# A transformer block in float32: the first stage's loads, warm-up and first tile rearranged

## The chip, the cores and the metric

The kernel runs on one core of a Trainium2 chip. A core has five engines that run side by side: TensorE (PE, matrix products into the accumulators in PSUM; its weight loads are shown apart as PEld), VectorE (DVE), ScalarE (ACT), GpSimd (POOL) and SyncE (SP, which here issues transfers). Sixteen DMA engines move data between the device's memory and the on-chip memory (SBUF). Each engine works through its own list of instructions in order, and waits on semaphores for the others. The metric is the device's time for one execution, in microseconds (us); smaller is better.

## The reference

The computation is linear attention without softmax, followed by an MLP mixer over tokens and then over channels. There are 8 batches, 8 heads, 576 tokens and 64 numbers a head; all is float32.

```python
kv = np.einsum('bhsd,bhse->bhde', k, v)
out = np.einsum('bhsd,bhde->bhse', q, kv)
rms = np.sqrt(np.mean(out * out, axis=-1, keepdims=True) + 1e-06)
attn = (out / rms * g_norm).astype(np.float32)

x = attn.transpose(0, 2, 1, 3).reshape(B, S, H * D)      # (8, 576, 512)
h = np.maximum(x.transpose(0, 2, 1) @ w_tok1, 0.0) @ w_tok2
u = x + h.transpose(0, 2, 1)
h2 = np.maximum(u @ w_ch1, 0.0) @ w_ch2
return (u + h2).astype(np.float32)
```

`w_tok1` is 576 x 256, `w_tok2` 256 x 576, `w_ch1` 512 x 1536, `w_ch2` 1536 x 512. The weights reach the kernel as pairs of 32-bit words for each number, and the kernel makes float32 of them ("decoding").

## The kernel before

The work has two parts. The first does attention and token mixing for pairs of batches, four pairs in all; the second does channel mixing, with products that are split further. The change touches only the first pair ("the first stage") and the loads ahead of it.

**The order is written out by hand.** Every instruction is recorded with `keep` (`tc.keep_in_program_order`), so each engine runs its instructions in the order in which the program issues them. That order comes from lists of short names: `start` for the first pair, `middle` and `steady` for the others. `play` (L1257) walks through the names and calls the function of each. The names that matter here, with S a batch of the pair (side), C a chunk of 256 tokens (0 and 1 of side 0, 2 and 3 of side 1, 4 the 64 last tokens of both), T one of its two tiles of 128 tokens, H a half:

- `kvSH` and `eSH` (L373, L387): k-by-v for four heads of one batch (20 products of 128x64, over five groups of rows), and its copy out of PSUM into `kvp`
- `aCT` (L395): one tile of q by kv, 4 products of 128x128; `a40` is the tile of the last tokens (`ps_r`)
- `gCT`, `qCT`, `tCH` (L444, L455, L469): times g into x (DVE), the square (ACT), the sum of squares of each head (DVE)
- `mC`, `rC`, `iC` (L477 to L493): mean, root and inverse for a whole chunk: on DVE, on ACT, and four small instructions on DVE
- `dCT`, `sCT` (L509, L502): x times the inverse, on DVE in one instruction or on ACT in eight
- `hSTj` (L541): x of group j times `w_tok1` (two weight passes of a 128x512 product each), for the first token product; `hr` adds the last tokens, `uN` is the second token product
- `wNK` (L162 to L192): decoding of block N in four steps: 1 on ACT (two instructions), 2, 3 and 4 on DVE. Blocks 0 and 1 hold groups 0, 1 and 2, 3 of `w_tok1`; block 2 its last rows; blocks 3 and 4 are `w_tok2`
- `lS`, `lqS`, `lrS`: the loads of the next pair; `jN` (L1341) N products on an identity matrix whose result nobody uses; `gs` (L1298) spreads g over the partitions with a product

A float32 product shows as two instructions of PE in the profile.

**Loads.** All go through `dma` (L123), nearly all on SyncE's queue. A load may be issued only when the load eight places earlier has landed. Before `start`, the program issues (L1276 to L1284): k of batch 0 on SyncE and v of batch 0 on ACT (each its rows, 1024 KB, and two remainders of 64 KB), q of batch 0 (`qT`, 1024 KB), blocks 0 and 1 of `w_tok1` (512 KB each), k and v of batch 1, q of batch 1, the last tokens of both q (`qR`), and the last rows of `w_tok1`. GpSimd sets the unused rows of k and v to zero (L1286) and then makes the identity; the row of g is loaded on ACT's queue (L1296).

**PSUM.** Three pools of 2 KB banks: `o` (2), `kv` (2) and `h` (4). In the first pair the two `kv` banks are set to zero and filled side by side (`zeroed`), the tiles of q by kv take `o`, and the accumulators of token mixing, the warm-up products and `ps_g` take `h`.

## Time and profile before

| | us |
|---|---|
| median of 3 runs (771.4 to 772.31) | 771.54 |
| the profiled execution | 771.12 |
| its span, first to last instruction | 769.3 |
| TensorE busy / idle in the span | 759.4 / 9.9 |
| DVE busy | 642.5 |
| ACT busy | 277.4 |
| first `ps_j` product / first `ps_kv` product | 3.34 / 8.81 |
| first `ps_g` / first `ps_o` / first `ps_h` product | 11.83 / 12.19 / 19.35 |
| first `ps_kv` product of batch 1 | 21.67 |
| first `ps_u` product | 47.20 |

The granted clock of TensorE is 0.999 over the span. The DMA engines are busy in over nine tenths of most slices of the first 80 us. The times of the rows in the lower half are from the profile's timeline, and count from the first instruction of the span.

### The profile page before, as it was taken

The numbers are of one execution on the slowest core, as the hardware profiler recorded it, in microseconds if no ns is written. First come the engines' busy times: TensorE is split into PE (matmuls) and PEld (weight loads), VectorE is DVE, ScalarE is ACT, GpSimd is POOL, SyncE is SP. The second block draws the span as 40 slices with busy tenths as digits, with TensorE's granted clock in tenths as the row PEclk, the third lists the DMA queues.
The fourth block names the chain that finished last, engine by engine and source line by source line (L and its number), as shares of the span: only waits on it lengthen the run. The fifth ranks groups of instructions, "written<-read, shape, count | busy, mean of one in ns | idle before, by whom it ended". The sixth has DMA issues, their size and how long they took to land.

```text
span 769.3 us, 12678 instructions
## 1 busy us (share of the span) xinstructions
PE 759.4 (99%) x4676; PEld 612.3 (80%) x4676; DVE 642.5 (84%) x945; ACT 277.4 (36%) x556; POOL 112.3 (15%) x125
## 2 busy tenths in 40 slices
PE   7999999999999999999999999999999999999998
PEld 6665555445888888888888888888888888888887
DVE  3868897997767779899969889987998996798996
ACT  3555575764210233511244242123352223325221
POOL 1003020213410000002240001042000218000204
PEclk9999999999999999999999999999999999999999
DMA  9999998499699786589998577999659879955679
GB/s 339 366 366 370 373 372 301 151 318 342 251 286 339 271 282 191 164 270 207 216 236 251 158 224 216 255 188 267 202 148 290 172 220 208 207 145 157 151 200 119
DMA packets 137677, 188.26 MB, mean 245 GB/s; under 512 B 48658, under 2 KB 95250, under 8 KB 135570
## 3 DMA queue, kind: packets, MB, share of 16 engines
q1 hardware_dynamic: 101744, 167.54, 68.9%
q0 software_dynamic: 34816, 18.36, 16.1%
q10 hardware_dynamic: 1058, 1.57, 0.6%
q8 instruction: 37, 0.61, 0.3%
q14 instruction: 22, 0.18, 0.1%
HBM read 138.28 MB, written 49.15 MB: 244 GB/s over the span
## 4 chain that ended last, share of the span: by engine, by line
PE 97%; DMA 2%; SPq 0%; issue 0%; DVE 0%
PE ps_d L136 28%; PE ps_b L136 19%; PE ps_a L136 19%; PE ps_u L136 8%; PE ps_h L136 8%; PE ps_v L136 5%; PE ps_c L136 3%; DMA v_in<-in_v_dram 2%; PE ps_kv L136 2%; PE ps_o L136 2%; PE ps_w L136 2%; SPq L124 0%; PE ps_r L136 0%; DVE xs L127 0%
## 5 line engine op out<-in xcount | busy, mean ns | idle before, releaser
L136 PE MATMUL ps_d<-ui,w 128*128 128x256 f32 x504 | 118.6, 379 | 0.0
L136 PEld LDWEIGHTS ps_d<-ui,w 128*128 128x128 f32 x504 | 95.9, 190 | 12.9
L133 ACT COPY ps_d<-ps_a 128x768 f32<-128x768 f32 (+1 forms) x56 | 32.0, 572 | 200.2 <-PE ps_a L136 197.2
L127 DVE TENSOR_TENSOR v<-v,v 128x1536 f32<-128x1536 f32 (+2 forms) x70 | 103.2, 1482 | 0.3
L136 PE MATMUL ps_b<-sv,w 128*128 128x256 f32 x324 | 78.9, 380 | 0.0
L136 PE MATMUL ps_a<-v,w 128*128 128x256 f32 x324 | 78.8, 379 | 0.0
L1206 POOL DMA_DIRECT2D out_dram<-us x24 | 26.7, 1833 | 291.8 <-ACT p L133 286.2
L136 PEld LDWEIGHTS ps_b<-sv,w 128*128 128x128 f32 x324 | 61.3, 190 | 8.8 <-issue 0.6
L136 PEld LDWEIGHTS ps_a<-v,w 128*128 128x128 f32 x324 | 61.7, 190 | 8.2
L136 PE MATMUL ps_u<-h,w_tok 128*128 128x512 f32 (+1 forms) x160 | 64.7, 599 | 0.0
L136 PE MATMUL ps_d<-v,w 128*128 128x256 f32 x258 | 62.7, 379 | 0.0
L130 ACT ACTIVATE v<-v 128x768 f32<-128x768 f32 (+1 forms) x54 | 42.6, 822 | 55.1 <-DVE v L127 52.3
L136 PE MATMUL ps_h<-x,w_tok 128*128 128x512 f32 x128 | 57.8, 600 | 0.7 <-DVE w_tok L190 0.7
L1206 POOL DMA_DIRECT2D out_dram<-r x40 | 41.3, 1927 | 102.0 <-ACT p L133 80.3
L136 PE MATMUL ps_d<-sv,w 128*128 128x256 f32 x228 | 55.4, 379 | 0.0
L136 PEld LDWEIGHTS ps_d<-v,w 128*128 128x128 f32 x258 | 49.0, 190 | 6.5
L136 PEld LDWEIGHTS ps_u<-h,w_tok 128*128 128x128 f32 (+1 forms) x160 | 25.6, 179 | 31.1 <-issue 26.7
L136 PEld LDWEIGHTS ps_d<-sv,w 128*128 128x128 f32 x228 | 43.4, 190 | 5.8
L136 PE MATMUL ps_a<-uT,w 128*128 128x256 f32 x192 | 46.7, 379 | 0.0
L136 PEld LDWEIGHTS ps_h<-x,w_tok 128*128 128x128 f32 x128 | 23.4, 190 | 27.1 <-issue 24.1
L136 PE MATMUL ps_b<-ui,w 128*128 128x256 f32 x168 | 40.8, 379 | 0.0
L136 PEld LDWEIGHTS ps_a<-uT,w 128*128 128x128 f32 x192 | 36.5, 190 | 4.9
(169 smaller groups left out, 1288.0 us busy)
## 6 DMA issues: line engine op xcount, KB each, us to landing
w<-parts SPq DMA_DIRECT2D x168, 384.0 KB
w<-parts SPq DMA_DIRECT2D x56, 192.0 KB
uT<-blocks SPq DMA_DIRECT2D x36, 256.0 KB
k_in<-in_k_dram SPq DMA_DIRECT2D x8, 1024.0 KB
qT<-in_q_dram SPq DMA_DIRECT2D x8, 1024.0 KB
out_dram<-x POOLq DMA_DIRECT2D x16, 512.0 KB, 7.0
v_in<-in_v_dram SPq DMA_DIRECT2D x7, 1024.0 KB
raw<-in_moe_w_ch_dram SPq DMA_DIRECT2D x8, 768.0 KB
```

The costliest lines, as they stand in the source:

```text
L127: keep(engine.tensor_tensor(out=o, in0=a, in1=b, op=op))
L130: keep(nc.scalar.activation(o, a, AF.Relu))
L133: keep(nc.scalar.copy(o, a))
L136: keep(nc.tensor.matmul(*a, **kw))
L1206: keep(nc.gpsimd.dma_start(to, t()[ds(b * Q, Q), at].rearrange("p n l j -> p n (l j)"), accum_op=ALU.add))
```

## The change

In the changed program:

- v of batch 0 is loaded on SyncE's queue too; for batch 0 the rows of k and v come first and the four remainders after them. g's row is loaded on GpSimd's queue, ahead of the memsets there. Block 0 of `w_tok1` is loaded and decoded in two halves (`first_rows`), the first right after batch 0 of k and v, the second after batch 1; block 1 follows the second half. q of batch 0 is loaded in two halves of 256 tokens.
- `kv00` and `kv01` are each split into the four groups of rows (`ka`) and the remainder (`kb`); `gs` stands between.
- The warm-up takes 21 products in place of 12, on a matrix of ones that DVE sets, and four more ahead of `a00`; the eight products ahead of `h000` are gone.
- The first tile's x no longer comes from `g00` and `d00`. kv times g is made on DVE for both halves (`eg0`, `eg1`), a product of q with it (`ag`) follows `a01`, and `dg` multiplies that by the inverse. The two tiles of chunk 0 have statistics of their own (`m00`, `r00`, `i00`; `m01`, `r01`, `i01`).
- `e01` moves from DVE to ACT; tile 1's scaling from ACT (`s01`) to DVE (`d01`), tile 11's from DVE (`d11`) to ACT (`s11`). Tiles `a30` and `a31` take the banks of `kv`, `a11` one of `h`. In the second half of `start` the products `h002`, `h012` come after `a31`.

```diff
-        queues = (nc.sync, nc.sync if b else nc.scalar)
-        for dst, t, e in zip((k_in[b % 2], v_in[b % 2]), (k, v), queues):
-            dma(dst[:, :J], t[b, :LO].rearrange("(p j) e -> p j e", j=J), e)
-            for n in range(0, HF, Q):
-                dma(dst[n:n + Q, J], t[b, LO + n:LO + n + Q].rearrange("(r e) d -> e r d", e=8), e)
+        pairs = ((k_in[b % 2], k), (v_in[b % 2], v))
+        if b:
+            for dst, t in pairs:
+                load_rows(dst, t, b)
+                load_rem(dst, t, b)
+        else:
+            for f in (load_rows, load_rem):
+                for dst, t in pairs:
+                    f(dst, t, b)
...
-            dma(qT[b], q[b].rearrange("(c p) s -> p c s", p=P)[..., :LO])
+            for n in range(0, LO, LO if b else LO // 2):
+                at = ds(n, LO if b else LO // 2)
+                dma(qT[b][..., at], q[b].rearrange("(c p) s -> p c s", p=P)[..., at])
...
+    def get_tok1_half(j):
+        return block(DTOK, lambda raw: [(raw, words(moe_w_tok1)[ts(j, P)])], w_tok1[0][:, j])
...
+        def evict_gain(half):
+            if not half:
+                sq["kvg"] = work.tile([P, H, D], F32, name="kvg", tag="sq", bufs=3)
+            keep(nc.vector.tensor_mul(sq["kvg"][:, 4 * half:4 * half + 4],
+                                      kv_ps[0, half].rearrange("p i (h d) -> p (i h) d", d=D),
+                                      g_sb.to_broadcast([P, 4, D])))
+
+        def attend_gain():
+            o = ps["h"].tile([P, DM], F32, name="ps_og", tag="h")
+            bank["g"] = o
+            for hp in range(HP):
+                matmul(o[:, ts(hp, P)], lhsT=qT[0][:, hp, ts(0, P)], rhs=sq["kvg"][:, 2 * hp:2 * hp + 2], start=True, stop=True)
 
         def attend_tile(c, t):
             side = c // 2
-            o = ps["o"].tile([P, DM], F32, name="ps_o", tag="o")
+            n = "kv" if c == 3 else "h" if (c, t) == (1, 1) else "o"
+            o = ps[n].tile([P, DM], F32, name="ps_o", tag=n)
...
+            if alone(c):
+                g = h
+                stat[g] = [stats.tile([P, H, 1], F32, name=name + str(h)) for name in ("ms", "root", "inv")]
+                keep(nc.vector.tensor_reduce(stat[g][0], sq[c, h], axis=AX.X, op=ALU.add))
+                return
...
+        def scale_first():
+            X[pair, 0] = xps[pair % 2].tile([P, 2, DM], F32, name="x", tag="x2", bufs=4)
+            of = lambda t: t.rearrange("p (k h d) -> p k h d", h=2, d=D)
+            keep(nc.vector.tensor_mul(of(X[pair, 0][:, 0]), of(bank["g"]), inv_of(0, 0).to_broadcast([P, HP, 2, D])))
...
+    first_rows = [get_tok1_half(j) for j in range(2)]
...
+    dma(g_row, bass.AP(tensor=g_norm.tensor, offset=g_norm.offset, ap=[[0, 1], list(g_norm.ap[0])]), nc.gpsimd)
     load(0)
+    first_rows[0][0]()
     load_q(0)
-    for block in tok1[:2]:
-        block[0]()
     load(1)
+    first_rows[1][0]()
+    tok1[1][0]()
     load_q(1)
...
+    keep(nc.vector.memset(ones, 1.0))
...
-        "j12 kv00 e00", "kv01 gs e01 l0", "a00 g00 q00", "a01 g01 q01 t00 t01 m0 w01",
-        "a10 w02 r0 i0 w03 d00 w04 q10 w30 w40 lq0", "a11 q11 s01 g10 g11 w11 j8",
-        "h000 h010 w12 w13 w14 t10 t11 m1 r1", "kv10 e10", "kv11 e11 i1 d10 d11 l1", "h001", "a20 q20", "h011",
-        "a21 q21 g20 g21 t20 t21 m2", "h002 h012 r2", "a30 g30 i2 d20 q30", "a31 q31 s21 g31 t30",
+        "j21 ka00 ka01 gs kb00 e00 kb01 e01 eg0 eg1 l0 w01 w02 w03 w04 j4",
+        "a00 q00 t00 m00 r00 i00", "a01 q01", "ag dg g01 t01 m01", "a10 q10", "a11 q11 r01 i01 w51 d01 w52 w53 w54",
+        "w30 w40 lq0 h000 h010", "kv10 e10 g10", "kv11 e11 g11 w11 t10 t11 m1 r1 w12 w13 i1 w14 d10 l1", "h001", "a20 q20", "h011",
+        "a21 q21 s11", "a30 q30", "a31", "h002 h012 g20 g21 t20 t21 m2 r2 i2 d20 g30 q31 s21 g31 t30",
         "h003 h013 t31 m3",
         "a40 q40 r3 i3 d30 s31 g40 t40 m4 r4 w21 i4 d40 lr0 lr1"]
...
     def keep_warm(n):
 
-        o = ps["h"].tile([P, DM], F32, name="ps_j", tag="h")
+        if n > 4:
+            late["junk"] = ps["h"].tile([P, DM], F32, name="ps_j", tag="h")
         for _ in range(n):
-            matmul(o[:, :P], lhsT=ident, rhs=ident, start=True, stop=True)
+            matmul(late["junk"][:, :P], lhsT=ones, rhs=ones, start=True, stop=True)
```

More of the change, by code (lines that the diff above doesn't have):

```diff
@@ L9 @@
 from concourse.dve_ops import ADD32_U16LIMBS
-from concourse.masks import make_identity
 F32 = mybir.dt.float32
@@ L97 @@
           for n, b in (("o", 2), ("kv", 2), ("h", 4))}
-    ident = inp.tile([P, P], F32, name="ident")
+    ones = inp.tile([P, P], F32, name="ones")
     g_sb = inp.tile([P, 1, D], F32, name="g_sb")
-    g_row, ones = (inp.tile([1, n], F32, name=name) for n, name in ((D, "g_row"), (P, "ones")))
+    g_row = inp.tile([1, D], F32, name="g_row")
     w_tok1 = [tokw.tile([P, 2, DTOK], F32, name=f"w_tok1{i}") for i in range(J // 2)]
@@ L139, with load_rows, load_rem @@
     qT, q_rest = {}, {}
+    def load_rows(dst, t, b):
+        dma(dst[:, :J], t[b, :LO].rearrange("(p j) e -> p j e", j=J))
+    def load_rem(dst, t, b):
+        for n in range(0, HF, Q):
+            dma(dst[n:n + Q, J], t[b, LO + n:LO + n + Q].rearrange("(r e) d -> e r d", e=8))
     def load(b):
@@ L164, in decode, with high, low, scale @@
         bits = dst.bitcast(U32)
-        def scale():
+        def high():
             keep(nc.scalar.activation(dst, raw()[..., 1].bitcast(F32), AF.Prelu,
                                       scale=2.0 ** -112, alpha=2.0 ** 32))
-            low = raw()[..., 0]
-            keep(nc.scalar.activation(low, low, AF.Copy, scale=2.0 ** -29))
+        def low():
+            t = raw()[..., 0]
+            keep(nc.scalar.activation(t, t, AF.Copy, scale=2.0 ** -29))
+        def scale():
+            high()
+            low()
         def scale_leaves():
@@ L190, in add @@
             keep(nc.vector._custom_dve(ADD32_U16LIMBS, out=o, in0=o, in1=flat().bitcast(U16)[..., 2 * leaves:][..., :2]))
-        return scale_leaves if leaves else scale, clamp, shift, add
+        return scale_leaves if leaves else scale, clamp, shift, add, high, low
     def words(w):
@@ L371, in attention, with kv @@
         whole = pair == 0
-        def kv(side, half):
+        def kv(side, half, js=range(JJ)):
             kk, vv = k_in[side], v_in[side]
-            if whole:
+            if js[0]:
+                o = kv_ps[side, half]
+            elif whole:
                 o = kv_ps[side, half] = zeroed[half]
@@ L378, in kv @@
                 o = kv_ps[side, half] = ps["kv"].tile([P, 2, P], F32, name="ps_kv", tag="kv")
+            split = len(js) < JJ
             for i in range(2):
-                for j in range(JJ):
+                for j in js:
                     for h in range(2):
@@ L384, in kv @@
                                rhs=vv[:, j, at],
-                               start=(j == 0), stop=(j == JJ - 1), skip_group_check=True)
+                               start=(j == 0 and not (split and i)), stop=(j == JJ - 1), skip_group_check=True)
         def evict(side, half):
@@ L389, in evict @@
             o, i = kvp[side][:, 2 * half:2 * half + 2, :n], kv_ps[side, half][:, :, :n]
-            if whole and side == 0:
+            if whole and side == 0 and half == 0:
                 keep(nc.vector.tensor_copy(o, i))
@@ L460, in group @@
             return next(g for g in groups if c in g)
+        alone = lambda c: whole and c == 0
         def stats_of(c):
@@ L495, in inv_of @@
         def inv_of(c, t):
+            if alone(c):
+                return stat[t][2].rearrange("p (k h) o -> p k h o", h=2)
             inv = stats_of(c)[2]
@@ L519, in attention @@
             for h in range(2):
-                steps |= {f"kv{s}{h}": do(kv, s, h), f"e{s}{h}": do(evict, s, h),
+                steps |= {f"ka{s}{h}": do(kv, s, h, range(J)), f"kb{s}{h}": do(kv, s, h, range(J, JJ)),
+                          f"kv{s}{h}": do(kv, s, h), f"e{s}{h}": do(evict, s, h),
                           f"l{s}": do(load, 2 * pair + 2 + s)}
@@ L532, in attention @@
                 steps |= {f"{n}{c}{t}": do(f, c, t) for n, f in zip("spd", (scale, scale_pool, scale_vector))}
+        if whole:
+            for h in range(2):
+                steps |= {f"m0{h}": do(mean, h), f"r0{h}": do(sqrt, h), f"i0{h}": do(invert, h)}
+                steps |= {f"eg{h}": do(evict_gain, h), "ag": attend_gain, "dg": scale_first}
         for g in groups:
@@ L1250, in stream @@
         for n in range(len(blocks)):
-            clamp, shift, add = blocks[n][2:]
+            clamp, shift, add = blocks[n][2:5]
             if n + 1 < len(blocks):
@@ L1293 @@
     keep(nc.scalar.activation(root, root, AF.Sqrt))
-    make_identity(nc, ident)
-    keep(nc.gpsimd.memset(ones, 1.0))
-    dma(g_row, bass.AP(tensor=g_norm.tensor, offset=g_norm.offset, ap=[[0, 1], list(g_norm.ap[0])]), nc.scalar)
     def spread_g():
         o = ps["h"].tile([P, DM], F32, name="ps_g", tag="h")
-        matmul(o[:, :D], lhsT=ones, rhs=g_row, start=True, stop=True)
+        matmul(o[:, :D], lhsT=ones[:1], rhs=g_row, start=True, stop=True)
         copy(g_sb[:, 0], o[:, :D])
     start = [
[4 rows of a table removed]
[4 rows of a table added]
         "h003 h013 t31 m3",
@@ L1333 @@
     mixings.append(token_mixing(B // 2 - 1, range(2, 9), (0, 1)))
-    more = {f"w{n}{k}": f for n, b in enumerate(tok1 + tok2) for k, f in enumerate(b)}
+    more = {f"w{n}{k}": f for n, b in enumerate(first_rows[:1] + tok1[1:] + tok2 + first_rows[1:]) for k, f in enumerate(b)}
     more |= {f"f{n}": b[0] for n, b in enumerate(channel)}
@@ L1341, in keep_warm @@
     def keep_warm(n):
-        o = ps["h"].tile([P, DM], F32, name="ps_j", tag="h")
+        if n > 4:
+            late["junk"] = ps["h"].tile([P, DM], F32, name="ps_j", tag="h")
         for _ in range(n):
-            matmul(o[:, :P], lhsT=ident, rhs=ident, start=True, stop=True)
-    more |= {f"j{n}": do(keep_warm, n) for n in (8, 12)}
+            matmul(late["junk"][:, :P], lhsT=ones, rhs=ones, start=True, stop=True)
+    more |= {f"j{n}": do(keep_warm, n) for n in (4, 5, 21)}
     more["gs"] = spread_g
```

## The prediction

> **What bounds the kernel now.** I read the page's first part and its chain of work first, then the same chain cut to the first 60 us, then what TensorE waited for over the whole span.

> ```profile
> PE   759.4 (99%) x4676; PEld 612.3 (80%) x4676; DVE 642.5 (84%) x945; ACT 277.4 (36%) x556; POOL 112.3 (15%) x125
> ...
> PE 97%; DMA 2%; SPq 0%; issue 0%; DVE 0%
> ...
> 0.75 7.97 DMA v_in<-in_v_dram
> ...
> 11.65 9.89 DMA v_in<-in_v_dram
> 21.54 0.14 issue
> 21.67 2.55 PE ps_kv L136 x80
> 24.23 1.06 PE ps_h L136 x2
> 25.28 1.09 PE ps_o L136 x8
> ...
> PE ps_j L136 <- POOL ident masks.py:199: 3.3, 1, 3.3
> PE ps_kv L136 <- DMA v_in<-in_v_dram: 1.5, 3, 0.8
> PE ps_h L136 <- DVE w_tok L190: 0.7, 1, 0.7
> PE ps_o L136 <- ACT sq L457: 0.6, 1, 0.6
> ```

> TensorE is the bound, and all its waits (6.1 us) lie before 21.67 us. From there to the end it never waits, so the time is settled by when this dense part begins. The chain says what lets it begin: not TensorE's early work but the landing of the second v (v1) at 11.65 + 9.89 = 21.54. All that TensorE does earlier (warm-up, kv of k0 and v0, tiles a00 to a11, two ps_h products) hangs beside that chain.

> Next I looked at what could bind soon after v1: the second q (qT1), which a20 needs. Its landing shows on SyncE, which may issue a load only when the load eight places earlier is down; v2's rows wait for qT1:

> ```profile
> 21.64 2.09 SPq L124 DMA_DIRECT2D k_in<-in_k_dram  x3
> 25.12 2.39 SPq L124 DMA_DIRECT2D v_in<-in_v_dram  x3
> ...
> SPq L124 <- DMA qT<-in_q_dram: 1.4, 1, 1.4
> ...
> 25.21 0.97 PEld L136 LDWEIGHTS ps_o<-kvp,qT 128*128 128x128 f32 x8 [0.76 <-ACT kvp L133]
> ```

> The first two lines are SyncE's timeline, the third its waits from 23.4 to 25.5 us, the last the timeline at a20. SyncE waited 1.4 us for qT and went on at 25.12; a20's weights began to load at 25.21. (The line puts the wait on ACT's copy of kvp, done by 24.63; the later release is qT1.) So a20 stands at two limits at once: v1 plus the products before it, and qT1's landing at about 25.1. This decides the case.

> The transfers themselves, in stretches (the last two numbers: busy share of the DMA engines, GB/s):

> ```profile
> 1.50:3.00 1.50, 0.00 (x0) 0.00 (x0) 0.00 (x0) 0.00 (x0) 1.37 (x5) 1.00 0.72 153
> 3.00:7.50 4.50, 4.16 (x22) 4.16 (x23) 0.00 (x0) 1.49 (x2) 0.43 (x2) 1.00 1.01 404
> 10.00:14.00 4.00, 4.00 (x82) 3.87 (x79) 1.39 (x3) 0.21 (x1) 0.00 (x0) 1.00 1.02 325
> 14.00:20.00 6.00, 4.73 (x37) 4.11 (x36) 5.66 (x15) 5.53 (x16) 0.00 (x0) 1.00 1.01 410
> 22.00:25.00 3.00, 3.00 (x79) 2.38 (x74) 2.55 (x9) 0.85 (x3) 0.00 (x0) 1.00 1.18 273
> ```

> From 3 us to 25 us the engines are full: nothing arrives earlier except by changing places with something else.

> **The change, part by part.** *Loads.* Sizes from the page: 1024 KB of rows and 2 x 64 KB of remainder for each k or v, 1024 KB a qT, 512 KB a block of w_tok1. Before, v1 ends after 2304 (k0, v0) + 1024 (qT0) + 1024 (two blocks) + 2304 (k1, v1) = 6656 KB, and qT1 after 7680. In the changed program's order on SyncE v1 ends after 2304 + 256 (half a block) + 1024 + 2304 = 5888 KB; then come half a block, a whole block and qT1, which again ends after 7680. So v1 comes 768 KB (786 kB) earlier: 1.95 us at 404 GB/s, 2.4 at 325. I take 1.95, since the window just ahead of it runs at 410: v1 at 19.6, bounds 19.1 to 19.6. qT1 stays at 25.1, because the same bytes lie ahead of it. qT0 now goes in two halves, whose contiguous pieces are half as long. No row times such pieces. Lower bound 0 (same bytes); upper, the fall from 404 (long pieces) to 325 GB/s (pieces of qT and w_tok1) once more, to 261: 1049 kB take 4.0 instead of 3.2 us, +0.8. I take 0.1, as both rows show full engines. A gain is possible too: see the first rival.

> v0 moves from ACT's queue behind k0 on SyncE's. Its rows issue about 0.45 us later (three k issues took 2.07 us), but k0 then has the engines to itself and the remainders no longer come between. The 2097 kB of rows: 230 kB by 3.0 us, the rest at 404 GB/s, so 7.6, and 7.9 with 0.3 for landing, against 0.75 + 7.97 = 8.72. g_row moves to GpSimd's queue, ahead of the four memsets there; those end about 2 us later, near 5, and are needed at 10. The page's GpSimd transfers land 5.7 to 7.1 us after issue, so g_row lands near 8 and is first used at 9.9.

> [...]

> *TensorE's early work.* Warm-up: 42 passes in place of 24, started by a memset on DVE near 1.1 instead of GpSimd's identity at 3.34. Before, 24 passes took 4.62 us; passes ran at 213 ns until 6.7 us and at 111 later. If the switch again takes 3.4 us, 42 passes end at 1.1 + 3.4 + 26 x 0.111 = 7.4; if it waits until 6.7, at 8.4. Then kv of the rows (64 passes, 2.0 us as at 9.82 to 11.83) 7.9 to 9.9; ps_g 0.36; remainders 16 passes, 0.5, to 10.75; four warm-up products 0.9 to 11.65; a00 and a01 1.78 (the row at 14.83) to 13.4; the new product with kv times g, 8 passes, 0.9, to 14.3; a10 and a11 to 16.1.

> Tile 0's own statistics: a00 is complete at 12.75; square 0.60, reduce 0.68, then mean, root and inverse 1.42 (23.39 to 24.81 before) to 15.55; one scaling straight from the new product, 0.69, to 16.3. The two kv-times-g multiplies (half of a 0.69 tile each) are done by 11.9, and the half decode (0.29 + 0.29 + 0.43) by 13.0, both beside TensorE's work. So h000 starts at 16.35 instead of 19.35: 3.0 us earlier, done at 18.1.

> *Where these 3 us go.* kv10 waits for v1 until 19.7 (idle 1.6), ends at 22.2, h001 (0.86) at 23.1. Then a20 waits for qT1 until 25.2 (idle 2.1). From a20 on both programs have the same products up to h100 (16 of ps_o, 8 of ps_r, 5 of ps_h), only in another order. The part that never waits thus starts at 25.2 to 25.3, where it started before.

> *DVE and ACT behind it.* Costing these at nothing needs cover. DVE's d10 comes after w11 on ACT, itself behind the copy of kv11 (done 22.7): w11's first half 23.4, w12 and w13 to 24.7, inverse 25.7, w14 26.4, d10 27.1. From there to the last decode of w_tok2 DVE has 8 multiplies (5.5), 5 reduces (3.2), 3 statistics (4.3) and decodes (1.2 + 1.85 + 1.85), together 17.9, plus about 1.2 us in which tile 2's root waits on ACT behind s11, now ACT's, and q30: 46.2. TensorE's u0 needs it at 47.2. Before, that decode ended at 44.89: the cover shrinks from 2.3 to 1.0 us. If it went, each missing us would be added to the time. PSUM: a30 and a31 take kv's banks, free since the copies at 22.7; the next kv needs them at 37.9, and DVE reads a31 by 34.9.

> *Sum.* Waits before 21.67: -3.0 us of early work, given back as 1.6 + 2.1 of new waits; later qT1 +0.1. Span 769.3 + 0.1 = 769.4. The profiled execution took 771.12, 1.8 more than its span: 771.2. The median of the runs shown, 771.54, is 0.4 above it, so as a median 771.6; as a gain on qT1 is likelier than a larger loss, I say 771.5.

> **The rivals.** *The transfers run better.* qT1's landing includes the two stretches at 325 and 273 GB/s. If the first does not recur, 1.30 MB at 404 take 0.8 us less; if the second does not, 0.82 MB take 1.0 less. Then qT1 lands at 23.3 and a20 follows h001 directly. For it: the order changes just there. Against: the blocks of w_tok1 and the short rows of qR, which stand in those stretches, move along with qT1. The gain is 0.9 to 1.9 us, more than the cover of 1.0 left by DVE only if v1, and so DVE, comes earlier too: 769.7 (-1.8).

> *The clock falls (slower).* Place: the two new waits of 1.6 and 2.1 us before kv10 and a20. If TensorE returns to 213 ns a pass for the 3.4 us that it took to leave it, 1.7 us of work are lost: 773.2. It decides from the idle time at which the clock is taken back. Known rows: idle 0.85 us at 7.96 left passes at their fast rate. For it: the waits are over twice as long; against: 3.4 us of work lie between them.

> [...]

> *It does not do what it says.* g_row lands late on GpSimd's queue and holds the remainders of kv. That counts only past 13.5 us (1.6 + 2.1 us of cover): twice its expected time. With other late loads behind the halves of qT0: 773 or more.

> **How the numbers follow.** qT1 binds, no change: 0.63, at 771.5 (own range 770.4 to 772.6: +-0.8 for qT1, +-0.3 for the runs). Transfers run better: 0.21, 769.7. Clock: 0.11, 773.2. Late loads: 0.05. A measurement of this kernel tells about 0.2% (1.5 us) from no change, so faster is below 770.0: three quarters of the better-transfers case and a little of the first, 0.18. Slower is above 773.1: 0.11 + 0.05 + 0.02 = 0.18. Same: 0.64. The range takes in part of both sides: 769.8 to 773.2.

> **What would show it.** Right: ps_h first at about 16.4; ps_kv of the second pair released by v_in near 19.6; TensorE idle some 2 us before a20; SyncE's wait for qT ending near 25.1; then no wait up to the end. Wrong: a20 well before 24 (then transfers ran better, and I look for a wait at u0 on DVE); passes of 213 ns after 18 us (clock); ps_kv or ps_g held past 10 us by g_row.

## The result and the profile after

The changed kernel takes 773.78 us (median of 13 executions, 771.93 to 776.54) against 771.40 (13 executions, 770.91 to 772.86) for the kernel before: ratio 1.0024, 95% interval 1.0014 to 1.0035. It is slower, by some 1.9 us by this ratio of all executions and by 2.4 us between the medians (the executions fall into groups, see below). The median is above the predicted range (769.8 to 773.2).

The profiled execution took 774.07 us with a span of 772.0, against 771.12 and 769.3. First the page's busy time and chain:

```profile
PE 763.5 (99%) x4694; PEld 615.0 (80%) x4694; DVE 643.8 (83%) x954; ACT 278.3 (36%) x560; POOL 112.2 (15%) x123
...
PE 96%; DMA 3%; DVE 0%; SPq 0%; issue 0%
```

TensorE has only 18 passes more but is busy 4.1 us longer. Its waits over the whole span (us in total, times, longest):

```profile
PE ps_o L135 <- DMA qT<-in_q_dram: 2.1, 1, 2.1
PE ps_j L135 <- DVE ones L1348: 1.1, 1, 1.1
PE ps_kv L135 <- DMA v_in<-in_v_dram: 0.4, 1, 0.4
PE ps_h L135 <- DVE w_tok L208: 0.2, 1, 0.2
```

The waits fell from 6.1 to 3.8 us, and the largest is the predicted one for qT1, to the tenth. TensorE's timeline (start, length, instructions, and in brackets the idle time before them and what ended it) shows the same:

```profile
16.82 1.98 PE L135 MATMUL ps_h<-x,w_tok 128*128 128x512 f32 x4
19.22 2.77 PE L135 MATMUL ps_kv<-v_in,k_in 128*64 128x64 f32 x80 [0.41 <-DMA v_in<-in_v_dram]
22.16 1.12 PE L135 MATMUL ps_h<-x,w_tok 128*128 128x512 f32 x2 [0.18 <-DVE w_tok L208]
25.39 1.50 PE L135 MATMUL ps_o<-kvp,qT 128*128 128x128 f32 x8 [2.10 <-DMA qT<-in_q_dram]
26.69 1.91 PE L135 MATMUL ps_h<-x,w_tok 128*128 128x512 f32 x2
28.39 3.33 PE L135 MATMUL ps_o<-kvp,qT 128*128 128x128 f32 x24
```

a20 starts at 25.39, 0.15 us later than in the kernel before (25.24). So far nothing is lost. But two passes of ps_h take 1.91 us here against 1.12 at 22.16: from a20 on TensorE works at about half speed. The stretches of the timeline (after the times and the busy time of TensorE and its weight loads come DVE, ACT, GpSimd, then the granted clock, DMA share and GB/s) name the reason:

```profile
19.16:22.58 3.42, 3.18 (x81) 2.85 (x82) 2.30 (x6) 1.60 (x5) 0.00 (x0) 1.00 1.06 372
22.58:25.99 3.41, 1.31 (x7) 0.63 (x6) 3.27 (x10) 1.16 (x3) 0.00 (x0) 1.00 1.17 271
25.99:29.40 3.41, 3.41 (x12) 2.38 (x12) 2.17 (x5) 0.60 (x1) 0.00 (x0) 0.50 0.99 318
29.40:32.82 3.42, 3.42 (x24) 2.73 (x23) 2.05 (x4) 2.79 (x10) 0.00 (x0) 1.00 1.01 404
```

The clock stands at 0.50 from 25.99 to 29.40, 3.41 us, and at 1.00 before and after. The stretches are cut where this profile's clock records change: it rose at 5.51 us, fell at 25.99, six steps of 3.413 us later, and rose again at 29.40, one step on. In the stretch that ends where the clock falls TensorE was busy for 1.31 of 3.41 us, 38%.

Lining up the products of both profiles gives the account of the 2.67 us by which the span grew: 0.15 at a20; 1.67 more by ps_r (35.09 against 33.27), about half of 3.41; nothing from there to the last product (767.11 against 765.27); and 0.83 behind the last product, where the span goes on for 4.58 us in place of 3.75. Another 0.28 lies outside the span (2.10 in place of 1.82 between span and execution).

In that end SyncE's stores wait longer for each other. Of SyncE's waits in the last nine us, the one for an earlier store of xg lasts at most 2.0 us, where the kernel before had 1.1 in its last nine (the first line is the changed kernel's, the second that of the kernel before):

```profile
SPq L123 <- DMA out_dram<-xg: 2.9, 2, 2.0
SPq L124 <- DMA out_dram<-xg: 1.6, 2, 1.1
```

### The profile page after: what moved, and what is told of

The parts are those of the page before. It is cut to its first block, busy times and chain, and to the rows that moved or that the text cites. A ratio compares the mean times of both kernels' runs of the same rounds, so it can differ in the third digit from the quotient of the medians.

```text
span 772.0 us, 12727 instructions
## 1 busy us (share of the span) xinstructions
PE 763.5 (99%) x4694; PEld 615.0 (80%) x4694; DVE 643.8 (83%) x954; ACT 278.3 (36%) x560; POOL 112.2 (15%) x123
## 4 chain that ended last, share of the span: by engine, by line
PE 96%; DMA 3%; DVE 0%; SPq 0%; issue 0%
PE ps_d L135 28%; PE ps_b L135 19%; PE ps_a L135 19%; PE ps_u L135 8%; PE ps_h L135 8%; PE ps_v L135 5%; PE ps_c L135 3%; PE ps_o L135 2%; PE ps_w L135 2%; PE ps_kv L135 2%; DMA qT<-in_q_dram 1%; DMA k_in<-in_k_dram 1%; DMA v_in<-in_v_dram 1%; PE ps_r L135 0%; DVE xs L126 0%; SPq L123 0%
## 5 line engine op out<-in xcount | busy, mean ns | idle before, releaser
L135 PEld LDWEIGHTS ps_h<-x,w_tok 128*128 128x128 f32 x128 | 23.7, 192 | 27.1 <-issue 24.6
```

What stands on the lines that cost most here:

```text
L135: keep(nc.tensor.matmul(*a, **kw))
```

## The experiments

Theory: the 2.1 us of waiting in front of a20 leave one window of 3.41 us too empty, the clock is halved for the next, and 1.7 us of work are lost; the gain that v1 made is given back at qT1; the rest is the end. Rivals: the load order itself costs; the two waits cost by their length; the late end is a matter of the number of TensorE's instructions. The granted clock of every execution is known, so they can be counted too: a mean of 0.997 or less is taken here as "with a halved window", 0.998 or more as "without". One halved window takes 0.0022 off the mean (half of 3.41 in 772 us), and the half clock behind the last product, when TensorE has stopped (from 770.09 us in the profile above), counts in it too. So 0.998 is not certain: a profile without a halved window in its work has 0.998 (qT1 in two halves, below), and an execution of 773.80 us of the changed kernel at 0.998 may have one. Of 94 executions of the kernel before beside these experiments none has one.

**The changed kernel again.**

> The changed kernel once more. Theory: TensorE idles about 2.1 us before a20, and its clock is judged in stretches of 3.4 us that run on whatever the kernel does; so in some executions a stretch holds most of the idle time and the clock is halved for the next 3.4 us (+1.7 us), and in others not. Expected: runs in two heaps, about 772.2 and about 773.9; the profile shows either a halved clock between 22 and 33 us or none, and a20 at about 25.4 in both. Rival (a fixed cost of 2.4 us somewhere): one heap at 773.8.

Measured: 773.53 us, ratio 1.0019 (1.0008 to 1.0031). The profile repeats the first: rise at 5.20, wait for qT 2.0 us, a window that is 41% busy, clock halved from 25.68 to 29.09. Over both sets 9 of 23 executions have a halved window, median 773.96; the other 14 have a median of 772.54. So the fall doesn't come every time, and without it the kernel is still about 1 us slower.

**The wait filled, wholly and by half.** Unused products run ahead of a20, in its own bank, while qT1 is on its way (nine in the first kernel, four in the second):

```
+            for _ in range(9 if (c, t) == (2, 0) else 0):
+                matmul(o[:, :P], lhsT=ones, rhs=ones, start=True, stop=True)
             for hp in range(HP):
```

> Nine products that nobody uses stand ahead of a20 and fill the 2.1 us in which TensorE waited for qT1. Theory (halved clock): the clock stays, a20 still starts at 25.3 to 25.5, and the time falls to 771.5 if the late end of the last stores goes too (nine more products move the last transfer of instructions about 2 us earlier), 772.3 if not; the spread of the runs shrinks to that of before. Rival (DVE or late loads hold the work behind a20): nothing changes, 773.8.

> The changed kernel with four unused products ahead of a20, so that TensorE's wait for qT1 is about 1.1 us long in place of 2.1 (nine products fill it wholly). Theory (the clock is halved only after a window of 3.41 us in which TensorE was busy for less than about half): the emptiest window is now at least 60% busy, so no halved clock in any run, and TensorE 0.1 to 0.2 us behind the kernel before: 771.7 to 772.3 us, the rest being the end. If any wait of over 1 us could bring the clock down, about half of the runs still show 1.7 us more and the median is 773 or above.

Measured: 771.87 us with nine, ratio 1.0011 (1.0001 to 1.0020), a halved window in 0 of 11 executions; 772.09 with four, ratio 1.0014 (1.0004 to 1.0023), in 1 of 11 (that one took 775.47). Of the eleven with nine products one, of 774.10 us, stands at 0.998 and can't be told. TensorE's timeline with nine:

```profile
22.09 1.13 PE L135 MATMUL ps_h<-x,w_tok 128*128 128x512 f32 x2 [0.17 <-DVE w_tok L208]
23.05 2.17 PE L135 MATMUL ps_o<-ones 128*128 128x128 f32 x18
25.34 1.13 PE L135 MATMUL ps_o<-kvp,qT 128*128 128x128 f32 x8
26.31 1.02 PE L135 MATMUL ps_h<-x,w_tok 128*128 128x512 f32 x2
```

a20 starts no earlier, since qT1 is no earlier, but its eight passes take 1.13 us in place of 1.50 and the ps_h products 1.02 in place of 1.91. More work and 1.7 to 1.9 us less time in the medians: the fall of the clock is the main loss of the executions that have it, and the emptiness of the wait causes it (9 of 23 executions fall without the filling, 1 of 22 with it). On average the filling is worth less, 0.4 to 1.0 us by the ratios, as 9 falls of 1.7 us in 23 executions are (0.7 us). Half the filling does as well; 0.9 us of wait are left in its profile. That a wait of over 1 us is not enough by itself is shown by longer ones below.

**qT1 in two halves**, the first ahead of the second block of w_tok1. This takes the wait away and not only its effect (the lines that give `load_q` its halves are left out):

```
...
     first_rows[1][0]()
+    load_q(1, (0,))
     tok1[1][0]()
-    load_q(1)
+    load_q(1, (1,))
```

> qT1 is loaded in two halves, the first ahead of block 1 of w_tok1, the second behind it. Theory: the first half lands near 22.7, a20 follows h001 at 23.3 without idle time, the clock stays, and the product stream starts 1.9 us earlier than before; DVE's last w_tok2 decode, due near 45.8 where u0 stands at 45.3, gives up to 0.5 us back, and the late end of the stores 0.85: 770.8. Rival (DVE binds at once): the gain is given back in waits on DVE between h002 and u0, 772.3 with the late end.

Measured: 769.83 us, ratio 0.9979 (0.9970 to 0.9987), no halved window in 11 executions: faster than both kernels, and 1.0 us faster than expected: TensorE comes 2.2 us ahead and not 1.9, nothing is given back on DVE (u0 starts at 44.94, 0.7 us after the decode that it needs), and the end is 0.7 us longer and not 0.85. Its waits, and its timeline from v1 on:

```profile
PE ps_j L135 <- DVE ones L1350: 1.1, 1, 1.1
PE ps_kv L135 <- DMA v_in<-in_v_dram: 1.0, 2, 0.8
PE ps_h L135 <- DVE w_tok L209: 0.2, 1, 0.2
```

```profile
19.12 2.70 PE L135 MATMUL ps_kv<-v_in,k_in 128*64 128x64 f32 x80 [0.21 <-DMA v_in<-in_v_dram]
21.99 1.12 PE L135 MATMUL ps_h<-x,w_tok 128*128 128x512 f32 x2 [0.17 <-DVE w_tok L209]
22.95 1.05 PE L135 MATMUL ps_o<-kvp,qT 128*128 128x128 f32 x8
```

The wait for qT is gone; a20 follows at 22.95, and from there to the last product TensorE is 2.2 us ahead of the kernel before. So the 2 us that v1 gains were real, and in the changed kernel qT1 took them back.

**The kernel before with nine more unused products** in its early waits, where they can delay nothing:

> The kernel before with nine more unused products, laid in its waits before 21.7 us, so that TensorE has as many instructions as in the changed kernel. Theory (a 16 KB transfer of instructions now falls among the last stores and holds one DMA engine): the first 765 us are as before to 0.2, and the time from the last product to the end grows from 3.8 to 4.6 us: 772.2. Rival (the late end in the changed kernel's profile was chance): 771.4.

Measured: 771.77 us, ratio 1.0006 (0.9997 to 1.0015). The products run 0.16 us later, the end takes 4.32 us in place of 3.75. No more than 0.6 us comes of it, and that in the end, as the expectation has it for another instruction transfer (38 packets on q8, a queue of instructions, as in the changed kernel, in place of 37). In the time itself (expected 772.2) it isn't shown, as the interval takes in 1.

**The changed kernel with nine fewer** (a warm-up of 32 passes, and without the four products ahead of a00: "j16" for "j21", "j4" left out), and the same in the kernel with the two halves of qT1:

> The changed kernel with nine unused products less, nothing else. Theory: a20 still waits 2 us for qT1, the clock is halved for 3.41 us in most runs, and the end takes 3.75 us in place of 4.58: 772.9 to 773.2 us, 0.7 below the changed kernel. If the end has nothing to do with the number of instructions, 773.6.

> The kernel with qT1 in two halves, the first ahead of the second block of w_tok1, and nine unused products less, so that TensorE has as many instructions as in the kernel before (its warm-up is 32 passes in place of 42, and the four unused products ahead of a00 are gone). Theory (the end grows with TensorE's instructions, by one more transfer of 16 KB of instructions among the last stores): TensorE 2.2 us ahead of the kernel before as with the halves alone, and the end back at about 3.75 us from 4.46: 769.1 us, ratio 0.997. If the end has nothing to do with the number of instructions, 769.8, ratio 0.998. A shorter warm-up could also bring the clock's rise later, which would show as passes of 213 ns past 6 us and up to 1 us more.

Measured: 773.08 us, ratio 1.0018 (1.0010 to 1.0027), a halved window in 5 of 11 executions; and 770.10, ratio 0.9986 (0.9977 to 0.9994), none in 11. The ends take 4.02 and 4.33 us, not 3.75, but less than the 4.58 and 4.46 with the nine products. So the number of TensorE's instructions explains a part of the late end and not the whole of it, the median of 773.08 inside its bounds notwithstanding.

All the profiles together say which part. SyncE issues its last store 0.49 us after the last product in every profile with 4676 passes of TensorE (the kernel before, these two, and two more below) and in that with 4712 (nine products ahead of a20). In the eight with 4694 or 4702 it does so 0.93 to 1.42 us after, and in these alone a fetch of 16 KB of instructions on q8 begins 1.7 to 2.6 us before the last product ends. In the last 8 us of the changed kernel that fetch is the first line here; neither the kernel before nor the changed one with nine fewer has such a line there, and in the latter the wait for an earlier store of xg is back at 1.3 us (second line, its last nine us):

```profile
q8 instruction: 1, 0.02, 0.7%
SPq L123 <- DMA out_dram<-xg: 2.0, 2, 1.3
```

The other part lies behind the last landing: from there to the end of the span it takes 1.39 and 1.71 us in these two kernels, 1.56 in the changed one and 1.13 in the kernel before.

The first of these profiles tells more. One of the 16 DMA engines is behind: of qT1's sixteen parts fifteen are down by 24.94 us and the last at 27.08. TensorE waits 2.7 us for it, longer than in the changed kernel's profile, yet the clock holds. Its stretches of 3.41 us, in step with its clock's rise:

```profile
19.00:22.41 3.41, 1.90 (x58) 1.85 (x60) 0.98 (x3) 0.68 (x2) 0.00 (x0) 1.00 1.02 361
22.41:25.83 3.42, 1.97 (x31) 1.00 (x27) 3.24 (x8) 1.86 (x5) 0.00 (x0) 1.00 1.12 267
25.83:29.24 3.41, 2.02 (x12) 1.57 (x13) 2.96 (x10) 0.81 (x2) 0.00 (x0) 1.00 0.97 287
29.24:32.65 3.41, 3.41 (x27) 2.93 (x26) 2.35 (x4) 2.45 (x10) 0.00 (x0) 1.00 0.99 359
```

The border at 25.83 cuts the long wait in two: no window is under 56% busy, and the clock stays at 1.00. Length alone, then, does not decide.

**The former load order under the changed program:**

> The changed program with the loads in their former order and on their former queues, so v1 lands near 21.5 us and qT1 near 25.1. The early products are done as early as in the changed kernel, so TensorE waits about 3 us in one piece before kv of the second pair, and hardly before a20. Theory (a halved clock follows a window of 3.41 us in which TensorE is busy for less than about half): the wait of 3 us halves the clock for one window right behind it, products of 213 ns for 3.41 us between about 22 and 29 us, TensorE 1.7 us behind the kernel before, and with the late end (+0.8) 773.5 to 774 us. If the halved clock belonged to the wait at a20 itself, or to the new load order, there would be none here and the time would be 771.5 to 772.3.

Measured: 773.13 us, ratio 1.0023 (1.0010 to 1.0036), a halved window in 3 of 7 executions (774.08 to 774.73). The profiled one waited only 1.5 us ahead of the second kv, its emptiest window was 56% busy, and its clock held. The median misses the expectation by 0.4 us, as fewer executions fell than I had thought; but the halved windows come without the new load order too, where the wait stands, by that profile, ahead of kv and hardly at all ahead of a20.

**The new load order under the program before.**

> The kernel before with only the loads in their new order (and the queue of g); TensorE's early work and tile 0's statistics stay as they were, with a few unused products more in the warm-up. v1 then lands near 19.6 us, when TensorE has just finished its early work, and qT1 at 25.1 as ever. Theory: the load order alone gives nothing, since a20 still waits for qT1; TensorE idles about 0.7 us there, no window falls below half, no halved clock: 771.3 to 772.3 us. If earlier v1 were worth its 2 us by itself, 769.5; if the new order were what costs, 773 or more.

Measured: 778.54 us, ratio 1.0095 (1.0082 to 1.0108), 4 executions, all with a mean clock of 0.997 or less. All my numbers are missed, for a reason I had overlooked. TensorE's largest wait and the ACT instruction behind it:

```profile
PE ps_h L136 <- DVE w_tok L201: 5.1, 1, 5.1
```

```profile
20.61 0.66 ACT L177 ACTIVATE w_tok<-raw 128x512 f32<-128x512 f32 x1 [4.30 <-DMA raw<-in_moe_w_tok_dram]
```

The program before decodes the first block of w_tok1 whole, and in the new order its second half lands behind v1. ACT stands 4.3 us for it, and behind it tile 0's root. So the new load order needs the decode by halves, which the change brings along. A repaired kernel sends that block whole ahead of qT0:

> The kernel before, with the changed kernel's order of loads except that the first block of w_tok1 goes whole, ahead of qT0 (the kernel before decodes it whole for its first ps_h product). TensorE's program and tile 0's statistics as before. Theory: v1 lands near 20.2 us, qT1 at 25.1 as ever; TensorE waits 0.5 us for qT1 ahead of a20, no halved clock, no gain: 771.3 us, ratio 1.000. If an earlier v1 were worth its time by itself, 770.0 to 770.5.

Measured: 772.76 us, ratio 1.0023 (1.0014 to 1.0032). No gain, rather 1.4 us of loss (1.8 by the ratio). Its profile (an execution of 773.78) shows the same fault one block on: the second block of w_tok1 lands behind v1 now, ACT stands 2.4 us for it and DVE 2.5 us for ACT, ACT in turn 2.6 us for the statistics that DVE has behind that decode; ACT's copy of kvp, queued behind, comes only at 27.03, and a20 at 27.44. So the expected time was missed, and a clean test of the loads under the program before was not made.

**The slots at the end.** At its end SyncE runs nine waits for the DMA slots, one behind the other; in the profile of the kernel before it took 0.06 to 0.09 us from one to the next behind its last pause. In that of the changed kernel the last store sat in the sixth slot from the end and was down 1.56 us before the end, and the five steps behind it took 0.64 us, one of them alone 0.36; in the kernel before it sat in the last but one, 1.13 us before. Five (in the changed kernel) and four (in that with two halves of qT1) later loads of qT are cut in halves, so that the stores get other slots of the ring (shown for the changed kernel):

```
-            for n in range(0, LO, LO if b else LO // 2):
-                at = ds(n, LO if b else LO // 2)
+            w = LO // 2 if b != 1 and b < 7 else LO
+            for n in range(0, LO, w):
+                at = ds(n, w)
```

> The changed kernel with five later loads of qT in halves, so that the ring of slots is turned by five and the last store stands near the end of SyncE's final walk. Theory: the clock is halved in about half of the runs as in the changed kernel, and from the last landing to the end of the span it takes 1.1 to 1.2 us in place of 1.56: the median 0.3 to 0.5 below the changed kernel, 773.2 us, runs without a halved clock 771.7. If the slots have nothing to do with the end, 773.6 and 772.2.

> The kernel with qT1 in two halves, the first ahead of the second block of w_tok1, and four later loads of qT in halves too, so that four more DMAs go through the ring of slots. Theory: at its end SyncE walks over the slots in a fixed order, about 0.06 us each, and a last store in an early slot leaves it a walk of up to seven after that store is down; with the ring turned by four the last store stands near the end of the order. From the last landing to the end of the span 1.1 to 1.2 us in place of 1.7: 769.3 us, 0.5 below the 769.83 without. If the slots have nothing to do with the end, 769.8.

Measured: 772.03 us, ratio 1.0015 (1.0004 to 1.0025), and 769.98, ratio 0.9987 (0.9979 to 0.9996). In both profiles 0.92 us remain from the last landing to the end, in place of 1.56 and 1.44, and the whole end takes 3.99 us. So this piece of the end went with the slots. What it is worth in time is not shown: the second kernel is no faster than with its slots unturned (769.83). The first is lower by about the forecast amount or more within each group (771.85 in place of 772.54 without a halved window, 773.47 in place of 773.96 with one), but the executions of a group lie up to 2 us and more apart; that its median falls by 1.5 us and more is mostly because 4 of 12 executions have a halved window in place of 9 of 23, which may be chance.

These two profiles also give the clearest pair on the clock. The changed kernel with turned slots waits for qT as ever:

```profile
PE ps_o L135 <- DMA qT<-in_q_dram: 1.9, 1, 1.9
```

but its clock rose at 6.95 us, so the borders lie elsewhere, and the wait (23.1 to 25.0) is cut at 24.01, five steps of 3.413 us behind the rise:

```profile
20.60:24.01 3.41, 2.33 (x44) 1.36 (x39) 3.11 (x7) 2.21 (x6) 0.00 (x0) 1.00 1.10 351
24.01:27.43 3.42, 2.42 (x16) 1.97 (x17) 3.25 (x11) 0.81 (x2) 0.00 (x0) 1.00 1.12 234
27.43:30.84 3.41, 3.41 (x25) 2.69 (x24) 2.53 (x5) 2.85 (x10) 0.00 (x0) 1.00 1.01 408
```

Two windows of 68 and 71%, no fall: span 769.3, the same as the kernel before. The other kernel's profiled execution had late transfers and waited 1.95 us for v1, here wholly inside one window:

```profile
17.76:21.17 3.41, 1.46 (x15) 0.58 (x15) 1.85 (x7) 0.21 (x1) 0.00 (x0) 1.00 0.99 353
21.17:24.58 3.41, 3.41 (x69) 3.41 (x67) 1.88 (x5) 1.14 (x3) 0.00 (x0) 0.50 0.98 278
24.58:28.00 3.42, 3.42 (x28) 2.40 (x25) 3.25 (x11) 2.32 (x5) 0.00 (x0) 1.00 1.03 274
```

43% busy, and the next window ran at half the clock (0.50). Among the windows before 60 us of all profiles those of 0, 38, 41 and 43% were followed by a fall, those of 56% and more were not.

The ends of the profiles, where TensorE stops, bring the bounds closer. The first two lines are from the program before with the new loads, the other two from the changed kernel with qT1 in two halves:

```profile
771.28:774.69 3.41, 1.64 (x15) 1.45 (x13) 0.85 (x2) 0.00 (x0) 0.00 (x0) 1.00 0.67 177
774.69:776.98 2.29, 0.00 (x0) 0.00 (x0) 0.00 (x0) 0.00 (x0) 0.00 (x0) 1.00 0.18 58
762.06:765.47 3.41, 1.33 (x12) 1.14 (x11) 0.85 (x2) 0.00 (x0) 0.00 (x0) 1.00 0.56 151
765.47:767.85 2.38, 0.00 (x0) 0.00 (x0) 0.00 (x0) 0.00 (x0) 0.00 (x0) 0.50 0.22 71
```

A window of 48% busy left the clock at 1.00, one of 39% was followed by 0.50.

## Why the prediction was wrong

*v1 and what hangs on it: right.* kv of the second pair started at 19.22 where 19.6 was expected (bounds 19.1 to 19.6): the lower bound holds. The warm-up ended at 8.13 (8.4 in the second case named), h000 started at 16.82 (16.35), h001 ended at 23.28 (23.1). The wait ahead of kv was 0.4 us and not 1.6, since the four ps_h passes there ended at 18.8, not 18.1, and v1 was earlier.

*qT1 binds, v1's gain is given back: right, and the heart of the case.* a20 waited 2.10 us (2.1) to 25.39 (25.2). qT1 had the same bytes ahead of it. Moving half of it ahead of 512 KB of w_tok1 was worth 3.7 us against the changed kernel (769.83 and 773.53 on one chip).

*Cover on DVE: right in sign, mis-sized.* The last decode of w_tok2 that u0 needs ends 1.8 us before u0 in the changed kernel and in that with turned slots; forecast were 1.0. No profile shows a wait at u0.

*The step that failed* is the sum: "-3.0 us of early work, given back as 1.6 + 2.1 of new waits; later qT1 +0.1". A wait was priced at its own length alone, and the end at no change at all. (The first three terms as written make +0.7 and not nothing, as the 0.34 us of wait that stood ahead of kv10 before were not taken off and the four ps_h passes were priced at 1.75 us for 1.99; the forecast itself rests on a20's start.) The rival "the clock falls" had the right place and the right price (1.7 us; measured 1.67) and got 0.11, because I weighed each wait by its own length and took the work between them as an argument against. What went with a fall in the profiles was the busy share of a window of 3.41 us in step with the clock's rise, which came at another time in each (at 5.51 us in the changed kernel's, at 6.95 in that with turned slots): a wait of 1.95 us inside one window (43% busy) brought the fall, one of 2.7 us across a border (no window under 56%) did not. From the profile of before this could have been asked: a20 waiting from 23.1 to 25.2 leaves at most 1.3 us of work in a window that holds it, which is far below the 66% that its emptiest window after the rise still had (6.88 to 10.30 us, busy 66%, clock 1.00).

*A term was missing:* the end. "1.8 more than its span" assumed that what lies behind the last product stays. It grew by 0.83 us inside the span (0.43 in the walk over the slots, the rest because SyncE issues its last store 0.96 us after the last product in place of 0.49) and 0.28 outside it. The late store comes with the number of TensorE's instructions: nine more products in the kernel before brought 1.23 us, nine fewer in the changed kernel 0.49. How the fetch does it is only argued: one part of an earlier store of xg landed 1.2 us after the other fifteen, about when the 16 KB were fetched. Why the time outside the span grew is open.

*Which term weighs more.* Without a halved window the changed kernel takes 772.54 us, 1 us over the forecast of 771.5 and inside its range, about what the end is worth (0.83 + 0.28 us). The falls, 1.67 us each, come in 9 of 23 executions, some 0.7 us on average, and it takes both to leave the range.

*Open:* a further group of executions runs 1 to 2 us late with a full clock: 6 of the 14 executions of the changed kernel counted as without a halved window, and some 10 of 94 of the kernel before. One such profile shows one of the 16 DMA engines 1.4 to 2.1 us behind the others. What holds it up, and whether the new loads make it more frequent, was not settled. It adds to the distance between the medians.

## What to carry to other kernels

When a load is brought forward, find the next operand that the same engine will need and move it too, or the gain becomes a wait there; here half a load moved by one place turned ratios of 1.0024 and 1.0019 into 0.9979. The new wait of 2.1 us on TensorE cost its length and, in 9 of 23 executions, a halved window behind it, 1.67 us in the profiled one: ask how full the emptiest 3.41 us will be, wherever they begin, and fill them with unused products if real work can't go there (nine of them left 0 of 11 executions with a halved window). Look past the last product: with other DMAs the last store stood in the sixth slot from the end in place of the last but one (1.56 us to the end against 1.13), and with 18 passes more a fetch of 16 KB began 1.8 us before the last product ended, and the last store was issued 0.96 us after that product in place of 0.49.
